# Retention and a Mish block on one core: when the weight sums are made, which staging buffers they share, and where the first block's stores stand in the queue

## The chip, the core and the metric

The kernel runs on one core of a Trainium2 chip. The core has five instruction streams that work side by side and wait for each other through semaphores: TensorE (PE in the profile; its weight loads are shown as PEld), VectorE (DVE), ScalarE (ACT), GpSimd (POOL) and SyncE (SP). Here SP does nothing but issue transfers, and 16 DMA engines carry them. The metric is the device time of one execution in microseconds (us); smaller is better. A kernel's time is the median of its runs.

## The reference, cut to what matters

A retention layer (linear attention with a decay for each head) runs over 4 batches of 768 tokens, 8 heads of 64. Its output is the input of a block with two weight matrices and the activation Mish between them.

```python
gamma = 1.0 - 2.0 ** (-5.0 - np.arange(H))
for t in range(S):
    state = gamma * state + einsum('bhd,bhe->bhde', k[:, :, t], v[:, :, t])
    y[:, :, t] = scale * einsum('bhd,bhde->bhe', q[:, :, t], state)
x = y.transpose(0, 2, 1, 3).reshape(3072, 512)
h = x @ w_in                       # 512 x 2048
g = h * np.tanh(softplus(h))       # Mish
out = g @ w_out                    # 2048 x 512
```

## The kernel before, in words

**Tiling.** The 3072 tokens are 24 chunks of 128. In a chunk the retention is done as attention under a mask (scores, mask, times V) plus the contribution of a running state. The chunks go in blocks: block 0 has four, the ten others two each (`BLOCKS`, line 39). A block has three parts: the retention of its chunks gives x, transposed (`xts`); then come the products with w_in and Mish (g, by 128 of the 2048 columns); then the products with w_out, whose results go through an output tile `osb` to memory. The retention of the next block is threaded into the products of this one.

**Sums instead of products.** Blocks 2 to 10 do both large products with seven block products in place of eight, and block 1 does so for its first one. This needs sums of weight blocks, made once on DVE: `wsum` of w_in (eight instructions of 128x512, line 581) and `tmat` of w_out (eight of 128x1024, lines 542 to 545, four for each half). Each block also needs sums of its own x (`x_sums`, lines 588 to 595, four on DVE) and of its own g (`gsum`).

**Order.** The order on every engine is written out by hand: `first_block`, then for each later block a dictionary of steps (`steps_of_half` for block 1, `steps_of` for the others), and in plain loops a `plan` from a unit's number to the work behind it. DVE work that has no fixed place is put in a list `late` and taken off it one by one (`some_late`).

**The first block.** SP issues, in this order, Q, K and V of chunks 0 to 3, the four slices of w_in (L150), the first three quarters of w_out (L154), loads for chunks 4 and 5, the last quarter of w_out in two halves (L159), and on. All weights come as float32 into staging buffers and are cast to float16: w_in by DVE (L165; one half slice by POOL), w_out by DVE (L175), its last quarter by ACT (L173). From unit 2 to 15 the loop does products with w_in (L490), from 16 to 31 with w_out (L512). In the second half stand the casts of Q and V on POOL (L322, L331) and of K on ACT (L327) for the coming chunks; the transposes of chunks 4 and 5 on PE, copied out of PSUM by DVE (`turn`, L366 to L370), which the scores (L379) of those chunks need; the mask (L385) and the state (L405, L410).

**Staging buffers.** The pool `rn_wstage` has four buffers under the tag `wt`, 8 KB a partition each, handed out in turn: first Q, the four slices of w_in, the four quarters of w_out, `wsum`, two `tmat`, and one `gsum`. A new owner waits until its predecessor has been read. The pool `rn_g` has two buffers under the tag `g`, for the g of blocks 1 on, and two under `g0`, for block 0's.

**Stores.** `g2_out` (L516) copies a finished product into an `osb` tile (L521 on DVE, L519 on ACT) and puts its store on a list, `stores`; `store_due(now)` issues on SP whatever is due (L181). There are five `osb` buffers. Block 0 fills four of them. Its stores are all issued at the step `end` of block 1's first product, behind `turn_and_load(a)`, which issues a transposition by DMA (L344) and three loads (L132). After the transposition by DMA of a chunk, the loads of the chunk two further on follow.

The functions that the change touches, and their callers:

Of the kernel before, what the change touches and what calls it, by code (L numbers as in the profile page):

```python
# [9 lines left out]
FP16 = mybir.dt.float16  # L10
FP32 = mybir.dt.float32
# [5 lines left out]
def kernel(  # L17
# [9 lines left out]
    nc = tc.nc  # L27
    B, H, S, D = q.shape
    d_model, d_ff = moe_w_in.shape
    P = 128  # L30
# [10 lines left out]
    NFB = d_ff // P  # L41
    NBP = d_model // P
    NSL = 4
    FPS = NFB // NSL
# [20 lines left out]
    wstage = ctx.enter_context(tc.tile_pool(name="rn_wstage", bufs=3))  # L65
    gp = ctx.enter_context(tc.tile_pool(name="rn_g", bufs=2))
    hp = ctx.enter_context(tc.tile_pool(name="rn_h", bufs=1))
    op = ctx.enter_context(tc.tile_pool(name="rn_o", bufs=5))
# [28 lines left out]
    for c in range(2):  # L97
        t = tri_first[c * HB:(c + 1) * HB]
# [16 lines left out]
    xts, gts, wins, wouts, wtmps = {}, {}, {}, {}, {}  # L115
# [29 lines left out]
    def load_w(which, s):  # L145
        if which == "in":
            t = wstage.tile([P, NBP, TB], FP32, name="wi", tag="wt", bufs=4)
            n = TB // 2 if s < 2 else TB
            for o in range(0, TB, n):
                nc.sync.dma_start(t[:, :, o:o + n], win_ap[:, :, s * TB + o:s * TB + o + n])  # L150
        else:
            t = wstage.tile([P, FPS, d_model], FP32, name="wt", tag="wt", bufs=4)
            if s < NSL - 1:
                nc.sync.dma_start(t, wout_ap[:, s * FPS:(s + 1) * FPS])  # L154
        wtmps[which, s] = t
# [6 lines left out]
    def cast_win(s, half, eng):  # L162
        src = wtmps["in", s]
        t = cpool.tile([P, NBP, TB // 2], FP16, name=f"win{s}_{half}")
        eng.tensor_copy(t, src[:, :, half * (TB // 2):(half + 1) * (TB // 2)])  # L165
        wins[s, half] = t

    def cast_wout(s, on_act=False):
# [6 lines left out]
            nc.vector.tensor_copy(t, src)  # L175
        wouts[s] = t

    def store_due(now):
        while stores and stores[0][0] <= now:
            _, dst, osb = stores.pop(0)  # L180
            nc.sync.dma_start(dst, osb)  # L181

# [341 lines left out]

    def weight_sums(half):
        n, hf = NFB // 2, d_model // 2  # L530
        if half == 0:
            tmats.extend(
                wstage.tile([P, 2, n, hf], FP16, name="tmat", tag="wt", bufs=4)
                for _ in range(2))
        f = slice(half * FPS, (half + 1) * FPS)
        t1, t2 = tmats[0][:, 0, f], tmats[0][:, 1, f]
        t3, t4 = tmats[1][:, 0, f], tmats[1][:, 1, f]
        b11, b12 = wouts[half][:, :, :hf], wouts[half][:, :, hf:]
        b21, b22 = wouts[half + 2][:, :, :hf], wouts[half + 2][:, :, hf:]
        sub = ALU.subtract  # L540
        return [
            lambda: nc.vector.tensor_tensor(t1, b12, b11, op=sub),
            lambda: nc.vector.tensor_tensor(t2, b22, t1, op=sub),
            lambda: nc.vector.tensor_tensor(t3, b22, b12, op=sub),
            lambda: nc.vector.tensor_tensor(t4, b21, t2, op=sub),
        ]

    def room_for_sums():
        n = NFB // 2
        gsums.append(wstage.tile([P, 4, n, P], FP16, name="gsum", tag="wt", bufs=4))  # L550
        gsums.append(gp.tile([P, 4, n, P], FP16, name="gsum", tag="g0"))

    def sum_views(blk, f=slice(None)):
        s = gsums[blk % 2]
# [236 lines left out]
    def first_block():  # L791
        qf = load_first_q()
        for s in range(2):
            for nm in "kv":
                for half in range(2):
                    load_two(nm, s, half)
        nload[0] = CPB
        load_weights()
        xts[0] = xtp.tile([P, CPB, HP, C], FP16, name="xt")

        at = at_tile()
        spin_wide(at, HP)
        spin_wide(at, HP)
        spin(at, 8)
        tq = turn_first_q(qf, 0)
        spin_wide(at, 3)
        first_q_out(0, tq, nc.scalar)
        tq = [tq, turn_first_q(qf, 1)]
        cast_two("k", 0, 0)
        turn_two(0, 0)  # L810
        first_q_out(1, tq[1], nc.vector)
        turned_two(0, 0)
        cast_two("k", 0, 1)
        spin_wide(at, 3)
        scores_half(0, 0, at)
        mask_half(0, 0, at)
        turn_two(0, 1)
        turned_two(0, 1)
        for half in range(2):
            cast_two("v", 0, half)  # L820
        at = at_tile()
        spin_wide(at, 3)
        scores_half(0, 1, at)
        mask_half(0, 1, at)
        cast_two("k", 1, 0)
        turn_two(1, 0)
        turned_two(1, 0)
        cast_two("k", 1, 1)
        outer_first(0)
        state_first(0)  # L830
        at = at_tile()
        scores_half(1, 0, at)
        mask_half(1, 0, at)
        y = atps.tile([P, 2, HP, C], FP32, name="y_ps", tag="at")
        present_first(0, y, range(HP))
        turn_two(1, 1)
        turned_two(1, 1)
        state_first(1)
        past_first(1, y)
        xt_out(0, y, nc.scalar, 2)  # L840
        for half in range(2):
            cast_two("v", 1, half)
        cast_win(0, 0, nc.gpsimd)
        at = at_tile()
        scores_half(1, 1, at)
        mask_half(1, 1, at)
        y = atps.tile([P, 2, HP, C], FP32, name="y_ps", tag="at")
        outer_first(1)
        state_first(2)
        present_first(1, y, range(HP // 2))  # L850
        h_ps = [mmps.tile([P, 1, TB], FP32, name="h_ps", tag="mm") for _ in range(2)]
        first_g1(h_ps[0], 0, 0)
        present_first(1, y, range(HP // 2, HP))
        past_first(2, y)
        past_first(3, y)
        xt_out(2, y, nc.scalar)
        xt_out(3, y, nc.vector)
        first_g1(h_ps[1], 1, 0)
        cast_win(0, 1, nc.vector)
        for u in range(2):  # L860
            first_g1(h_ps[u], u, 1)
            mish(0, u, h_ps[u])
        state_first(3)
        for s in range(1, NSL):
            for half in range(2):
                cast_win(s, half, nc.vector)
        plan = {
            9: [(cast_wout, 0)],
            12: [(cast_wout, 1)],
            16: [(cast_wout, 2), (load_more,), (casts, CPB)],  # L870
            23: [(casts, CPB + 1), (cast_wout, 3, True)],
            24: [(turn, CPB)],
            25: [(scores_one, CPB)],
            27: [(turn, CPB + 1)],
            28: [(outer_state, CPB), (casts, CPB + 2), (turn_and_load, CPB + 2), (cast_q, CPB + 3)],
            29: [(scores_one, CPB + 1)],
            31: [(y_two, 1)],
        }
        o_tiles = [None] * CPB
        for u in range(2, 2 * NFB):  # L880
            if u < NFB:
                g1(0, u)
            elif u < 2 * NFB - 2:
                w = u - NFB
                for t in range(CPB):
                    if w == 0:
                        o_tiles[t] = mmps.tile([P, d_model], FP32, name="o_ps", tag="mm")
                    g2_mm(o_tiles[t], 0, t, w)
            else:
                for t in range(CPB // 2) if u % 2 == 0 else range(CPB // 2, CPB):  # L890
                    for w in range(NFB - 2, NFB):
                        g2_mm(o_tiles[t], 0, t, w)
                    g2_out(o_tiles[t], 0, t, 1, on_act=t == CPB - 1)
            for fn, *args in plan.get(u + 1, ()):
                fn(*args)
            if u == NFB + 1:
                late.extend(win_sums())
            if NFB < u <= NFB + 4:
                late.pop(0)()
                late.pop(0)()  # L900
            if u == NFB + 4:
                late.extend(weight_sums(0))
            if u in (NFB + 5, NFB + 8):
                late.pop(0)()
        hsnaps.append(gp.tile([P, 4, TB], FP32, name="hsnap", tag="g0"))

    def turn_and_load(g):
# [43 lines left out]
            "m3": only((x_sums, nb)),  # L951
        }

    def some_late(n):
        for _ in range(min(n, len(late))):
            late.pop(0)()

    def steps_of_half(blk):
        a = first[blk] + 4
        return {  # L960
            "p2": [(gate_x, blk), (cast_v, a - 1)],
            "u2": [(cast_k, a - 1)],
            "p6": [(turn_and_load, a - 1), (some_late, 1)],
            "p7": [(cast_q, a), (some_late, 1)],
            "p4": [(cast_v, a), (some_late, 2)],
            "end": [(cast_k, a), (turn_and_load, a), (store_due, 3)],
        }

    def plan_of(blk):
# [6 lines left out]

    first_block()
    x_sums(HALF_SEVEN)
    late.extend(weight_sums(1))
    room_for_sums()  # L980
    for blk in range(1, len(BLOCKS)):
        if blk >= SEVEN:
            steps = steps_of(blk)
# [50 lines left out]
```

## Time and profile before

| what | value |
|---|---|
| median of 3 runs | 204.72 us (204.32 to 204.83) |
| the profiled execution's own time | 204.39 us |
| its span in the profile | 202.6 us |
| busy: PE, PEld, DVE, ACT, POOL | 193.1, 152.6, 143.5, 111.3, 67.6 us |
| granted TensorE clock | 1.00 |
| moved by DMA | 38.65 MB, mean 191 GB/s |

The profile shows one execution, a little under the median of the runs. The span is what the engines' records cover; 1.79 us of the time lie around it. A line of a timeline gives the start, the duration, the engine, the line of the kernel, the operation, what is written and read, and in brackets how long the engine was idle before it and what ended that wait. The releaser is inferred: it is the last one that the profile shows, which can be wrong where a DMA was waited for as well. Durations of one engine overlap a little, because the next instruction starts before the last one's results have all arrived.

### The profile page before, as it was taken

What the parts mean: (1) busy time and instruction counts of PE and PEld (TensorE: products, weight loads), DVE (VectorE), ACT (ScalarE), POOL (GpSimd) and SP (SyncE); (2) the same over time, 40 slices, a digit from 0 to 9 for tenths busy, and PEclk for the clock granted to TensorE, in tenths of its full rate; (3) what the DMA queues carried; (4) which work ended last, traced back from release to release, by engine and by line L of the source; (5) the groups of instructions that cost most, each with busy time, mean ns of one, the idle gap of its engine ahead of it and who ended that gap; (6) DMA issues with size and microseconds to landing.
All of it is one profiled execution on the core that took longest, in us unless ns stands there. A gap on an engine that the chain in (4) does not pass through costs nothing.

```text
span 202.6 us, 5428 instructions
## 1 busy us (share of the span) xinstructions
PE 193.1 (95%) x2239; PEld 152.6 (75%) x2239; DVE 143.5 (71%) x271; ACT 111.3 (55%) x199; POOL 67.6 (33%) x83
## 2 busy tenths in 40 slices
PE   6788999989999899999999999999999999999993
PEld 2355444445865788988988988988988988988982
DVE  2786644988889587578596696787696696696552
ACT  2462764152970673774674674674674663753850
POOL 4072000607434236424407517604407616200000
PEclk9999999999999999999999999999999999999999
DMA  5999999999999999997991992999992952200202
GB/s 175 300 314 359 386 387 297 275 250 199 188 172 223 326 217 206 188 239 149 230 186 55 222 240 80 230 180 155 248 210 48 234 87 55 104 3 23 85 26 78
DMA packets 95896, 38.65 MB, mean 191 GB/s; under 512 B 82304, under 2 KB 89984, under 8 KB 95872
## 3 DMA queue, kind: packets, MB, share of 16 engines
q1 hardware_dynamic: 92608, 37.50, 82.8%
q10 hardware_dynamic: 3264, 0.82, 2.4%
q8 instruction: 17, 0.28, 0.6%
q14 instruction: 7, 0.06, 0.1%
HBM read 27.30 MB, written 6.29 MB: 166 GB/s over the span
## 4 chain that ended last, share of the span: by engine, by line
PE 76%; DMA 10%; SPq 6%; DVE 4%; ACT 1%; issue 1%
PE o_ps L714 28%; PE h_ps L643 18%; PE h_ps L619 16%; PE o_ps L512 6%; DMA wi<-in_moe_w_in_dram 5%; DMA wt<-in_moe_w_out_dram 5%; SPq L217 4%; PE y_ps L429 3%; PE at L379 3%; DVE wsum L581 3%; PE y_ps L419 2%; SPq L150 2%; PE u_ps L393 2%; ACT xt L475 1%; DVE win L165 1%
## 5 line engine op out<-in xcount | busy, mean ns | idle before, releaser
L643 PE MATMUL h_ps<-xt,win 128*128 128x256 f16 x320 | 41.2, 273 | 0.0
L322 POOL TENSOR_TENSOR qk<-qf,qvs 128x512 f16<-128x512 f32 x20 | 23.4, 1172 | 26.2 <-DMA qf<-in_q_dram 26.2
L643 PEld LDWEIGHTS <-win 128*128 128x128 f16 x320 | 29.4, 98 | 3.6
L714 PEld LDWEIGHTS <-gsum 128*128 128x128 f16 x288 | 27.5, 98 | 3.9
L636 DVE TENSOR_TENSOR hsum<-h_ps,hsnap 128x512 f32<-128x512 f32 x30 | 19.8, 688 | 13.5 <-PE h_ps L619 11.3
L647 ACT ACTIVATE g<-h_ps 128x512 f16<-128x512 f32 x40 | 23.7, 594 | 5.6 <-PE h_ps L643 5.5
L385 DVE TENSOR_TENSOR am<-at,tri 128x1024 f16<-128x1024 f32 x20 | 24.2, 1216 | 1.6 <-PE at L379 1.6
L714 PE MATMUL o_ps<-tmat,gsum 128*128 128x256 f16 x216 | 25.1, 273 | 0.0
L626 ACT COPY hsnap<-h_ps 128x512 f32<-128x512 f32 x30 | 16.6, 588 | 14.5 <-PE h_ps L619 14.5
L331 POOL TENSOR_TENSOR v<-vf,qvs 128x512 f16<-128x512 f32 x20 | 21.5, 1073 | 5.4 <-DMA vf<-in_v_dram 5.4
L714 PEld LDWEIGHTS <-g 128*128 128x128 f16 x216 | 21.1, 98 | 2.5
L728 DVE TENSOR_TENSOR osb<-o_ps,snap 128x256 f32<-128x256 f32 x27 | 11.4, 423 | 16.1 <-PE o_ps L714 11.7
L512 PE MATMUL o_ps<-wout,g 128*128 128x512 f16 x96 | 22.7, 380 | 0.0
L475 ACT CAST xt<-y_ps 128x1024 f16<-128x1024 f32 x10 | 10.1, 1012 | 19.7 <-PE y_ps L429 19.7
L630 ACT ACTIVATE g<-hsum 128x512 f16<-128x512 f32 x30 | 18.7, 634 | 4.0 <-DVE hsum L636 4.0
L619 PEld LDWEIGHTS <-wsum 128*128 128x128 f16 x320 | 19.1, 98 | 1.1 <-DVE xsum L593 0.6
L720 ACT COPY snap<-o_ps 128x256 f32<-128x256 f32 x27 | 10.1, 373 | 15.7 <-PE o_ps L714 15.7
L327 ACT ACTIVATE qk<-kf 128x512 f16<-128x512 f32 x20 | 12.7, 633 | 9.4 <-DMA kf<-in_k_dram 5.0
L714 PE MATMUL o_ps<-wout,g 128*128 128x256 f16 x144 | 17.2, 273 | 0.0
L619 PE MATMUL h_ps<-xsum,wsum 128*128 128x128 f16 x240 | 16.7, 219 | 0.4 <-DVE xsum L593 0.4
L340 POOL COPY gate<-gsum 128x1 f16<-128x1 f16 x8 | 1.5, 188 | 44.0 <-DVE gsum L688 44.0
L619 PEld LDWEIGHTS <-win 128*128 128x128 f16 x240 | 15.1, 98 | 1.5 <-issue 0.8
(96 smaller groups left out, 288.5 us busy)
## 6 DMA issues: line engine op xcount, KB each, us to landing
kf<-in_k_dram SPq DMA_DIRECT2D x23, 256.0 KB, 3.9
vf<-in_v_dram SPq DMA_DIRECT2D x23, 256.0 KB, 5.5
out_dram<-osb SPq DMA_DIRECT2D x22, 256.0 KB, 4.3
qf<-in_q_dram SPq DMA_DIRECT2D x19, 256.0 KB, 4.4
wt<-in_moe_w_out_dram SPq DMA_DIRECT2D x3, 1024.0 KB, 8.8
wi<-in_moe_w_in_dram SPq DMA_DIRECT2D x4, 512.0 KB, 7.3
wi<-in_moe_w_in_dram SPq DMA_DIRECT2D x2, 1024.0 KB, 11.2
qfirst<-in_q_dram SPq DMA_DIRECT2D x2, 512.0 KB, 5.1
```

The lines of the kernel that those rows point to most:

```text
L322: nc.gpsimd.tensor_tensor(room16(g)[0], loaded[g][0], qs.unsqueeze(2).broadcast_to((P, H, D)), op=ALU.mult)
L327: nc.scalar.mul(room16(g)[1], loaded[g][1], BOOST)
L331: nc.gpsimd.tensor_tensor(room16(g)[2], loaded[g][2], vs.unsqueeze(2).broadcast_to((P, H, D)), op=ALU.mult)
L385: nc.vector.tensor_tensor(am, ats.pop(g), tri.unsqueeze(1).unsqueeze(1).broadcast_to((P, 2, HP, C)), op=ALU.mult)
L512: nc.tensor.matmul(o_ps, gts[blk, fb][:, t * P:(t + 1) * P], wouts[s][:, f, cols], start=(fb == 0), stop=(fb == NFB - 1))
L619: nc.tensor.matmul(h_ps[:, f], w(f, d), x(d), start=first and f == 0 and d == 0, stop=d == n - 1, skip_group_check=True)
L626: nc.scalar.copy(x, h_ps)
L630: nc.scalar.activation(gt[:, 2 * i * FPS:(2 * i + 1) * FPS, j * P:(j + 1) * P], h, AF.Mish, scale=inv_boost3)
L636: nc.vector.tensor_tensor(h, h_ps, x, op=ALU.add)
L643: nc.tensor.matmul(h_ps[:, j], win(s, 2 * half + j, bp), xt(blk, bp), start=bp == 0, stop=bp == NBP - 1)
L647: nc.scalar.activation(gt[:, fb:fb + 2], h_ps, AF.Mish, scale=inv_boost3)
L714: nc.tensor.matmul(o_ps, x(f), w(f), start=first and f == 0, stop=f == n - 1, skip_group_check=True)
```

## The change

In words:

- The eight sums of w_in (`wsum`) move from the second half of block 0 (units 17 to 20) to the casts of w_in: four behind slice 2, four behind slice 3. 
- The eight sums of w_out (`tmat`) start at unit 16: five of them in units 16 to 20 (before: one behind unit 21 and one behind unit 24), one at each of the steps `p6`, `p7` and `p4` of block 1 (before: four at these steps and two in the loop behind).
- Staging: quarters 2 and 3 of w_out are loaded into the two buffers `g` instead of `wt`. The order of owners in `wt` becomes first Q, four slices of w_in, two quarters of w_out, `wsum`, `gsum`, two `tmat`. The load of quarter 2 no longer waits for the cast of w_in's slice 2.
- Stores: block 0's four stores are issued two at step `p4`, ahead of `turn_and_load(a)`, and two behind it at step `end`, whatever their due number.

PE's instructions and their order stay as they were; POOL's and ACT's too. DVE's differ only by the moved sums, SP's by the two moved stores.

```diff
@@ load_w
-            t = wstage.tile([P, FPS, d_model], FP32, name="wt", tag="wt", bufs=4)
+            if s < NSL // 2:
+                t = wstage.tile([P, FPS, d_model], FP32, name="wt", tag="wt", bufs=4)
+            else:
+                t = gp.tile([P, FPS, d_model], FP32, name="wt", tag="g")
@@ stores
+    def store(n):
+        for _ in range(n):
+            _, dst, osb = stores.pop(0)
+            nc.sync.dma_start(dst, osb)
+
     def store_due(now):
         while stores and stores[0][0] <= now:
-            _, dst, osb = stores.pop(0)
-            nc.sync.dma_start(dst, osb)
+            store(1)
@@ sums
+    def some_late(n):
+        for _ in range(min(n, len(late))):
+            late.pop(0)()
...
     def room_for_sums():
         n = NFB // 2
         gsums.append(wstage.tile([P, 4, n, P], FP16, name="gsum", tag="wt", bufs=4))
-        gsums.append(gp.tile([P, 4, n, P], FP16, name="gsum", tag="g0"))
+
+    def room_for_more():
+        n, hf = NFB // 2, d_model // 2
+        tmats.extend(
+            wstage.tile([P, 2, n, hf], FP16, name="tmat", tag="wt", bufs=4) for _ in range(2))
@@ first_block
         for s in range(1, NSL):
             for half in range(2):
                 cast_win(s, half, nc.vector)
+            if s == 2:
+                late.extend(win_sums())
+            if s >= 2:
+                some_late(4)
+        room_for_sums()
...
-            if u == NFB + 1:
-                late.extend(win_sums())
-            if NFB < u <= NFB + 4:
-                late.pop(0)()
-                late.pop(0)()
-            if u == NFB + 4:
-                late.extend(weight_sums(0))
-            if u in (NFB + 5, NFB + 8):
-                late.pop(0)()
+            if u == NFB - 1:
+                room_for_more()
+                late.extend(weight_sums(0) + weight_sums(1))
+            if NFB <= u < NFB + 5:
+                some_late(1)
@@ steps_of_half
-            "p4": [(cast_v, a), (some_late, 2)],
-            "end": [(cast_k, a), (turn_and_load, a), (store_due, 3)],
+            "p4": [(cast_v, a), (some_late, 1), (store, 2)],
+            "end": [(cast_k, a), (turn_and_load, a), (store, 2)],
@@ behind first_block
     x_sums(HALF_SEVEN)
-    late.extend(weight_sums(1))
-    room_for_sums()
+    gsums.append(gp.tile([P, 4, NFB // 2, P], FP16, name="gsum", tag="g0"))
```

`weight_sums` computes the same four differences for a half as before; only its views are written as functions.

More of the change, by code (lines that the diff above doesn't have):

```diff
@@ L524, in g2_out, with t, b @@
         stores.append((due, dst, osb))
+    def some_late(n):
+        for _ in range(min(n, len(late))):
+            late.pop(0)()
     def weight_sums(half):
[L530 to L534, printed above, removed]
+        hf = d_model // 2
         f = slice(half * FPS, (half + 1) * FPS)
[L536 to L539, printed above, removed]
         sub = ALU.subtract
+        def t(i):
+            return tmats[i // 2][:, i % 2, f]
+        def b(i, j):
+            return wouts[half + 2 * i][:, :, j * hf:(j + 1) * hf]
         return [
[L542 to L545, printed above, removed]
+            lambda: nc.vector.tensor_tensor(t(0), b(0, 1), b(0, 0), op=sub),
+            lambda: nc.vector.tensor_tensor(t(1), b(1, 1), t(0), op=sub),
+            lambda: nc.vector.tensor_tensor(t(2), b(1, 1), b(0, 1), op=sub),
+            lambda: nc.vector.tensor_tensor(t(3), b(1, 0), t(1), op=sub),
         ]
@@ L952, in steps_of @@
         }
-    def some_late(n):
-        for _ in range(min(n, len(late))):
-            late.pop(0)()
     def steps_of_half(blk):
```

## The prediction

> **What bounds the kernel now.** I read the span first, then the engines' busy time by stretches, then what TensorE (PE) waited for, then the timeline around each such wait. In the rows by stretch the columns are: stretch, length, busy time (count) of PE, PEld, DVE, ACT and POOL, granted clock, DMA share, GB/s.
>
> ```profile
> span 202.6 us, 5428 instructions
> ...
> 20.00:33.00 13.00, 13.00 (x64) 6.08 (x63) 7.09 (x10) 8.86 (x16) 0.00 (x0) 1.00 1.06 381
> ...
> 40.00:46.00 6.00, 5.10 (x46) 2.83 (x44) 4.73 (x6) 2.72 (x3) 1.36 (x2) 1.00 1.20 252
> ...
> 67.00:75.00 8.00, 7.54 (x109) 6.76 (x109) 6.16 (x15) 5.86 (x11) 3.42 (x4) 1.00 1.17 279
> ...
> 90.00:190.00 100.00, 100.00 (x1274) 89.82 (x1273) 73.21 (x152) 59.65 (x111) 36.07 (x42) 1.00 0.74 146
> ```
>
> From 90 to 190 us PE never pauses, so only a pause that PE makes earlier can be won. The list of waits names two after 33 us, both on DVE:
>
> ```profile
> PE at L379 <- DVE qkt L370: 0.9, 1, 0.9
> PE h_ps L619 <- DVE xsum L593: 0.4, 1, 0.4
> ```
>
> The change touches both places. PE's own instructions stay the same, in the same order.
>
> **Sums of w_in, moved forward (eight wsum, L581).** They now stand behind the casts of slice 2 (four) and slice 3 (four).
>
> ```profile
> 20.71 12.25 PE L490 MATMUL h_ps<-xt,win 128*128 128x512 f16 x56
> 23.52 1.29 DVE L165 CAST win<-wi 128x1024 f16<-128x1024 f32 x2 [0.73 <-DMA wi<-in_moe_w_in_dram]
> 26.20 1.30 DVE L165 CAST win<-wi 128x1024 f16<-128x1024 f32 x2 [1.38 <-DMA wi<-in_moe_w_in_dram]
> 28.91 1.23 DVE L175 CAST wout<-wt 128x2048 f16<-128x2048 f32 x1 [1.42 <-DMA wt<-in_moe_w_out_dram]
> ...
> 34.45 1.23 DVE L175 CAST wout<-wt 128x2048 f16<-128x2048 f32 x1 [1.59 <-DMA wt<-in_moe_w_out_dram]
> 35.59 0.42 DVE L581 TENSOR_TENSOR wsum<-win 128x512 f16<-128x512 f16 x1
> ```
>
> One sum takes about 0.37 us from start to start (0.42 less the overlap), four about 1.5. DVE is idle for 1.38 us ahead of the casts of slice 3, and 1.42 ahead of wout0: the sums fill these gaps and push each cast by some 0.1. PE runs 56 matmuls from 20.71 in 12.25 us and wants slice 3 after 40 of them, at 29.5; its first cast ends near 27.0. So I take nothing. Bounds: a slowed sum takes 1.27 (below); four of those would end at 29.9 and the cast at 30.6, a PE pause of 1.1. POOL, which slows them, does nothing from 20 to 33 (row above), so I keep the low end.
>
> **Load of w_out's third part, no longer waiting for slice 2's cast.** SP may issue it up to 2 us sooner. But the rings are full from 20 to 33 us (share 1.06, 381 GB/s), one ring serves in order, and 1 MB at 381 GB/s is 2.75 us whenever it is queued. Gain 0; upper bound the 2 us that SP waited. The third cast then still starts at 34.45. The other shared buffers (sums, g) get earlier or equally early owners: their last readers are casts that DVE or ACT has done in block 0, before the next writer's turn. 0.
>
> **The first pause, 42 us.** Chunk 4's turned Q and K are copied by DVE (L370) before PE can score.
>
> ```profile
> 36.04 1.15 DVE L581 TENSOR_TENSOR wsum<-wsum,win 128x512 f16<-128x512 f16 x1
> 37.11 1.26 DVE L581 TENSOR_TENSOR wsum<-win,win 128x512 f16<-128x512 f16 x1
> ...
> 39.75 1.27 DVE L581 TENSOR_TENSOR wsum<-win,wsum 128x512 f16<-128x512 f16 x1
> 40.94 0.68 DVE L542 TENSOR_TENSOR tmat<-wout 128x1024 f16<-128x1024 f16 x1
> 41.54 0.68 DVE L370 COPY qkt<-t_ps 128x1024 f16<-128x1024 f16 x1
> ...
> 35.69 1.22 POOL L322 TENSOR_TENSOR qk<-qf,qvs 128x512 f16<-128x512 f32 x1 [19.04 <-DMA qf<-in_q_dram]
> 36.89 1.20 POOL L331 TENSOR_TENSOR v<-vf,qvs 128x512 f16<-128x512 f32 x1
> 39.64 1.10 POOL L322 TENSOR_TENSOR qk<-qf,qvs 128x512 f16<-128x512 f32 x1 [1.55 <-DMA qf<-in_q_dram]
> ...
> 40.12 0.39 PE L368 MATMUL t_ps<-ident,qk 128*128 128x128 f16 x4
> 40.34 1.03 PE L512 MATMUL o_ps<-wout,g 128*128 128x512 f16 x4
> 42.27 0.40 PE L379 MATMUL at<-qkt 64*128 64x128 f16 x8 [0.90 <-DVE qkt L370]
> ```
>
> PE's transposes end at 40.51, so the copy could start at 40.55 instead of 41.54, and PE score at 41.28 (0.73 after the copy's start, as 41.54 to 42.27): a gain of 0.99 if DVE is free by then. Eight wsum and one tmat leave the place behind the wout2 cast; five tmat take it. Free of POOL that is 5 x 0.6 = 3.0 us, done at 38.6.
>
> But the three long wsum are those that meet a POOL cast, and each ends 0.28 us after that cast (36.91 to 37.19, 38.09 to 38.37, 40.74 to 41.02): two-input DVE sums and POOL casts take turns. A tmat that waits so ends 0.28 + 0.27 (the doubled elements) = 0.55 after POOL. Played through: tmat 1 from 35.59 to 36.27, POOL's first cast to 37.18, tmat 2 to 37.73, POOL's second to 38.63, tmat 3 to 39.18, tmat 4 to 39.78; POOL's third arrives at 39.64, ahead of tmat 5, which starts near 39.7, so tmat 5 ends at 41.25. The copy starts at 41.17, PE at 41.90: gain 0.37. The bounds are 0 and 0.99, and some 60 ns at 39.64 decide; I take 0.37, since the rows show the turns.
>
> The Trainium skill, page "SBUF — State Buffer", section "Who interferes with whom", says that a DVE instruction with two SBUF inputs contends with a POOL instruction that reads SBUF, that the loser blocks for the whole instruction, and that issue order decides. By that rule, the first pause yields 0.37; without it, 0.99; the three long wsum agree with it.
>
> What follows a gain of 0.37:
>
> ```profile
> 46.37 1.04 POOL L322 TENSOR_TENSOR qk<-qf,qvs 128x512 f16<-128x512 f32 x1
> 46.80 1.16 DVE L410 TENSOR_TENSOR st<-su,gcm 128x512 f16<-128x512 f32 x1
> 47.88 1.21 DVE L385 TENSOR_TENSOR am<-at,tri 128x1024 f16<-128x1024 f32 x1
> 49.44 0.64 PE L429 MATMUL y_ps<-am,v 128*64 128x128 f16 x16
> ```
>
> The state update L410 waits for the POOL cast of 46.37 already; issued 0.37 sooner, at 46.43, it still does, so the mask behind it ends at 49.09 as before. PE would want it at 49.07 instead of 49.44, and gets it at 49.13 (0.04 to hand over). So 0.31 of the 0.37 stays.
>
> **The second pause, 69 us: the stores.** The output tiles (osb) have five buffers; block 0 takes four and block 1's second tile takes the first again, so its copy (L521) waits until the first store has landed.
>
> ```profile
> 63.44 0.85 SPq L181 DMA_DIRECT2D out_dram<-osb  x1
> out_dram<-osb SPq DMA_DIRECT2D x1, 256.0 KB, 4.2
> ...
> 65.84 1.04 PE L512 MATMUL o_ps<-wout,g 128*128 128x512 f16 x4
> 66.86 0.63 ACT L327 ACTIVATE qk<-kf 128x512 f16<-128x512 f32 x1
> 67.66 0.59 ACT L626 COPY hsnap<-h_ps 128x512 f32<-128x512 f32 x1 [0.17 <-PE h_ps L619]
> 67.69 0.69 DVE L521 COPY osb<-o_ps 128x512 f32<-128x512 f32 x1 [1.76 <-PE h_ps L619]
> 67.90 0.61 PE L393 MATMUL u_ps<-v,qk 128*128 128x128 f16 x8
> 68.96 1.07 PE L619 MATMUL h_ps<-xsum,wsum 128*128 128x128 f16 x16 [0.45 <-DVE xsum L593]
> ```
>
> The row puts the copy's wait down to PE, but 63.44 + 4.2 = 67.64 is the store, and DVE starts 0.05 later. Behind the copy stand the x sums, and PE waits for the second of them until 68.96. Its previous work, eight matmuls from 67.90 (0.45 at their spacing), lets it go on at 68.35: 0.61 to win. The new order issues the first two stores right after chunk 9's loads:
>
> ```profile
> 57.93 1.00 SPq L132 DMA_DIRECT2D vf<-in_v_dram  x1
> 59.18 1.84 SPq L344 DMA_TRANSPOSE qkt<-qk  x1
> 61.07 0.58 SPq L132 DMA_DIRECT2D kf<-in_k_dram  x1
> kf<-in_k_dram SPq DMA_DIRECT2D x1, 256.0 KB, 3.7
> ```
>
> That is near 59.0, landing near 63.2, over 3 us before block 1's last tile. The copy then starts when PE's last four matmuls end (66.88). From the copy's start to PE's it is 1.27 (67.69 to 68.96), so the sums are there at 68.15 and PE goes on at 68.35. I take 0.61; bounds 0 and 0.61.
>
> What pays are the queue's later entries: the transpose of chunk 8 (59.18) and chunk 10's three loads (from 61.07) each go behind two stores, 0.5 MB or some 1.2 us (four stores take 2.41 us of SP, half of them 1.2). The transpose is not needed before the next block's scores, past 73 us. Chunk 10's K is needed sooner: ACT casts it (L327, 66.86) straight ahead of the snapshot L626 that PE needs. It lands at 61.07 + 3.7 = 64.77 now. With 1.2 more it is 65.97, against a cast that is wanted at 66.55 after the first gain: hidden, with 0.6 to spare.
>
> The three tmat left for block 1 stand where six stood: 0.
>
> **The sum.** 204.39 (the profiled execution: span 202.6 and 1.79 around it) - 0.31 - 0.61 = 203.47. The median of the runs shown, 204.72, is 0.33 above that execution, which makes 203.80 at the median; the runs lie from 204.32 to 204.83, so I forecast between the two scales, 203.6.
>
> **The rivals.**
>
> *DVE gets past POOL.* If tmat 5 is issued before POOL's third cast (its Q lands 0.1 us later, or DVE runs 0.1 ahead), the first pause goes almost whole: 0.99 + 0.61 = 1.60, 202.8 on the profile's scale, 203.1 at the median. For it: only 60 ns are missing. Against it: the order is set by a DMA landing that the change does not touch. Chance 0.25.
>
> *Half comes.* The gain of one place only: tmat 5 caught for longer, or chunk 10's K landing between 66.6 and 67.8 and holding the snapshot. Gain 0 to 0.6, so 204.1 to 204.7. For it: the turns with POOL are tight, and the queue's backlog grows by two stores. Chance 0.22.
>
> *Chunk 10's K too late.* Its cast blocks ACT, the snapshot L626 starts 0.55 after the cast, and PE goes on 0.63 after that: landing + 1.18. From a landing of 67.8 on, PE starts no sooner than 68.96, and both gains are gone. Issued at 62.3 (61.07 + 1.2), it needs 5.5 us for that; 6.1 us makes 68.4 and +0.6, that is 205.0 (205.3 at the median). For it: the queue is full there. Against it: this load takes 3.7 now. Chance 0.08.
>
> **How the numbers follow.** The forecast has 0.45. A difference under 0.3% (0.61 us) can't be told from none here. Forecast and the first rival are faster, and a little of the second: 0.72. Most of the second is within: 0.19. The late K is slower, with what I have not thought of: 0.09. The range goes from the first rival on the profile's scale, 202.8, to well into the second, 204.5.
>
> **What would show it.** Right: no osb copy (L521) that waits over 1 us, first stores near 59, PE's wait at L619 gone, L379 reached near 41.9 with tmat 5 ending near 41.2, and the later blocks shifted as a whole. L379 at 41.3 is the first rival. Wrong: a DMA wait of ACT's K cast near 66 us with PE waiting for the snapshot; slice 3 cast after 29.5; the wout2 cast away from 34.4; a new PE pause between 46 and 67.

## The result, and the profile after

| | before | after |
|---|---|---|
| median | 204.72 us (203.76 to 205.47, 22 runs) | 203.91 us (203.0 to 204.49, 22 runs) |
| ratio after/before, 95% interval | | 0.9966 (0.9952 to 0.9979) |
| the profiled execution's own time | 204.39 us | 203.41 us |
| its span | 202.6 us | 201.2 us |

The changed kernel is faster by some 0.3%. The rows by stretch of the changed kernel, with the same columns as in the prediction:

```profile
40.00:46.00 6.00, 6.00 (x50) 3.17 (x48) 3.76 (x5) 2.48 (x3) 1.56 (x2) 1.00 1.19 251
67.00:75.00 8.00, 8.00 (x112) 7.25 (x110) 6.50 (x15) 5.91 (x11) 3.42 (x4) 1.00 1.11 253
```

PE is busy through both stretches (5.10 of 6.00 us and 7.54 of 8.00 before), and its list of waits holds nothing at L386 and L632, which are lines 379 and 619 of before. The timeline up to the first place (lines 168 and 178 are DVE's casts of w_in and w_out, 551 to 554 are the `tmat` sums, before 542 to 545; 377 is the copy, before 370; 329 and 338 are POOL's casts, before 322 and 331):

```profile
26.36 1.30 DVE L168 CAST win<-wi 128x1024 f16<-128x1024 f32 x2
29.08 1.23 DVE L178 CAST wout<-wt 128x2048 f16<-128x2048 f32 x1
...
34.60 1.23 DVE L178 CAST wout<-wt 128x2048 f16<-128x2048 f32 x1 [1.59 <-DMA wt<-in_moe_w_out_dram]
36.46 1.42 DVE L552 TENSOR_TENSOR tmat<-wout,tmat 128x1024 f16<-128x1024 f16 x1
37.80 1.53 DVE L553 TENSOR_TENSOR tmat<-wout,wout 128x1024 f16<-128x1024 f16 x1
39.25 0.68 DVE L554 TENSOR_TENSOR tmat<-wout,tmat 128x1024 f16<-128x1024 f16 x1
39.85 0.68 DVE L551 TENSOR_TENSOR tmat<-wout 128x1024 f16<-128x1024 f16 x1
40.40 0.39 PE L375 MATMUL t_ps<-ident,qk 128*128 128x128 f16 x4
40.52 1.04 POOL L329 TENSOR_TENSOR qk<-qf,qvs 128x512 f16<-128x512 f32 x1 [1.74 <-DMA qf<-in_q_dram]
40.82 0.69 DVE L377 COPY qkt<-t_ps 128x1024 f16<-128x1024 f16 x1 [0.29 <-PE t_ps L375]
41.58 0.40 PE L386 MATMUL at<-qkt 64*128 64x128 f16 x8
```

The second and third `tmat` take turns with POOL's casts as forecast (1.42 and 1.53 us instead of 0.68). The fifth takes only 0.68: in this execution POOL's third cast, which waits for its Q to land, starts at 40.52, where the profile of before had it at 39.64. PE's last transposes start 0.28 us later here than before (40.40 against 40.12), and the scores come at 41.58. So the profile shows the first rival, "DVE gets past POOL" (it had the scores at 41.28), while the median lies beside the forecast's own sum. That contradiction was the question for the experiments.

The second place, by the timeline of the changed kernel:

```profile
57.68 1.77 SPq L184 DMA_DIRECT2D out_dram<-osb  x2
...
66.16 0.63 ACT L334 ACTIVATE qk<-kf 128x512 f16<-128x512 f32 x1
66.22 0.69 DVE L528 COPY osb<-o_ps 128x512 f32<-128x512 f32 x1 [0.98 <-PE o_ps L519]
67.20 0.61 PE L400 MATMUL u_ps<-v,qk 128*128 128x128 f16 x8
67.65 1.06 PE L632 MATMUL h_ps<-xsum,wsum 128*128 128x128 f16 x16
```

The copy of the output tile (L528, before L521) waits for PE alone now, and PE goes from L400 to L632 without a pause.

### The profile page after: what moved, and what is told of

Its sections match the earlier page's. It is cut to its first block, busy times and chain, and to the rows that moved or that the text cites. A ratio compares the mean times of both kernels' runs of the same rounds, so it can differ in the third digit from the quotient of the medians.

```text
span 201.2 us, 5425 instructions
## 1 busy us (share of the span) xinstructions
PE 193.6 (96%) x2239; PEld 152.5 (76%) x2239; DVE 142.3 (71%) x271; ACT 111.2 (55%) x199; POOL 68.1 (34%) x83
## 4 chain that ended last, share of the span: by engine, by line
PE 91%; ACT 2%; DMA 2%; DVE 2%; issue 1%; DVEq 0%
PE o_ps L727 28%; PE h_ps L656 18%; PE h_ps L632 16%; PE o_ps L519 10%; PE h_ps L497 6%; PE y_ps L436 3%; PE at L386 3%; DMA qfirst<-in_q_dram 2%; PE y_ps L426 2%; PE u_ps L400 2%; ACT xt L482 1%; PE h_ps L800 1%; DVE qfirst L204 1%; DVE am L274 1%; ACT qk L235 1%
## 5 line engine op out<-in xcount | busy, mean ns | idle before, releaser
L329 POOL TENSOR_TENSOR qk<-qf,qvs 128x512 f16<-128x512 f32 x20 | 24.1, 1207 | 25.3 <-DMA qf<-in_q_dram 23.4
L741 DVE TENSOR_TENSOR osb<-o_ps,snap 128x256 f32<-128x256 f32 x27 | 11.4, 424 | 16.1 <-PE o_ps L727 11.3
L632 PEld LDWEIGHTS <-wsum 128*128 128x128 f16 x320 | 19.1, 98 | 0.5
L632 PE MATMUL h_ps<-xsum,wsum 128*128 128x128 f16 x240 | 16.7, 219 | 0.0
L632 PEld LDWEIGHTS <-win 128*128 128x128 f16 x240 | 15.1, 98 | 1.5 <-issue 0.8
```

The costliest lines, as they stand in the source:

```text
L329: nc.gpsimd.tensor_tensor(room16(g)[0], loaded[g][0], qs.unsqueeze(2).broadcast_to((P, H, D)), op=ALU.mult)
L632: nc.tensor.matmul(h_ps[:, f], w(f, d), x(d), start=first and f == 0 and d == 0, stop=d == n - 1, skip_group_check=True)
```

## The experiments

Three readings of each trace do most of the work, and need a word first. The *chain* is the time from the start of DVE's cast of w_out's third quarter (34.45 before, 34.60 after) to PE's first scores of chunk 4: DVE's work in between and, where DVE is done early, the wait for PE's transposes. The *turn* is the time from PE's transposes (L375) to those scores: PE's own view. The *second stretch* is the time from those scores to the first matmul on `xsum` (L632). What follows after that is the same in all: from L632 to the end of the span are 133.5 to 133.7 us (202.6 - 68.96 before, 201.2 - 67.65 after). Experiments are measured beside the kernel before on the same chip, on three chips in all, on which the kernel before has medians of 204.64, 204.81 and 204.89; so kernels of different chips are compared by their ratios. The columns in the middle come from the one profiled execution each, worked out from its rows.

| kernel | third POOL cast | chain | turn | second stretch | span | median of runs (range, runs) | ratio to before (95%) |
|---|---|---|---|---|---|---|---|
| before | 39.64 | 7.82 | 2.15 | 26.69 | 202.6 | | |
| after | 40.52 | 6.98 | 1.18 | 26.07 | 201.2 | 203.91 (203.0 to 204.49, 22) | 0.9966 (0.9952 to 0.9979) |
| stores_only | 40.38 | 7.22 | 1.18 | 26.08 | 201.4 | 203.91 (203.08 to 204.47, 12) | 0.9960 (0.9936 to 0.9984) |
| six_osb | 39.81 | 7.83 | 2.40 | 26.08 | 202.4 | 204.22 (202.97 to 204.48, 12) | 0.9975 (0.9954 to 0.9996) |
| sums_only | 39.69 | 7.44 | 1.73 | 27.05 | 202.8 | 204.85 (204.03 to 205.32, 12) | 1.0003 (0.9982 to 1.0023) |
| load_only | 39.82 | 7.83 | 2.43 | 26.85 | 203.3 | 204.96 (204.44 to 205.44, 12) | 1.0013 (0.9996 to 1.0031) |
| four_stores_early | 39.58 | 7.43 | 1.65 | 26.07 | 201.6 | 204.00 (203.32 to 205.29, 12) | 0.9976 (0.9951 to 1.0002) |
| after_again | 39.49 | 7.44 | 2.09 | 26.07 | 201.8 | 203.92 (203.74 to 204.84, 12) | 0.9972 (0.9955 to 0.9989) |
| four_first | 39.88 | 6.09 | 1.18 | 26.08 | 200.9 | 203.15 (202.75 to 203.57, 8) | 0.9931 (0.9901 to 0.9960) |
| pool_gate | 40.87 | 6.89 | 1.18 | 26.08 | 201.3 | 203.24 (202.81 to 203.29, 6) | 0.9927 (0.9904 to 0.9949) |
| four_old_stores | 39.43 | 6.54 | 1.18 | 27.03 | 201.8 | 203.91 (203.63 to 203.99, 5) | 0.9949 (0.9931 to 0.9967) |
| stores_gate | 41.01 | 6.98 | 1.46 | 26.08 | 201.2 | 203.11 (203.08 to 203.29, 4) | 0.9916 (0.9892 to 0.9939) |

**The stores alone** (stores_only). The kernel before, with the new order of the stores and nothing else of the change.

```diff
-            "p4": [(cast_v, a), (some_late, 2)],
-            "end": [(cast_k, a), (turn_and_load, a), (store_due, 3)],
+            "p4": [(cast_v, a), (some_late, 2), (store, 2)],
+            "end": [(cast_k, a), (turn_and_load, a), (store, 2)],
```

> The kernel before, with only the stores of block 0 issued two by two. My theory: the copy L521 waits for the landing of the first store, so its idle 1.8 us goes, PE's 0.45 us wait for the x sums at 69 us goes, and the first pause (PE at L379 waiting for the copy L370 near 42 us) stays: 0.6 us less than before, ratio 0.997. Rival (the row is right, the copy waits for PE): nothing changes, ratio 1.000. Rival (chunk 10's K comes too late behind the stores): ACT's cast near 66 us waits for a DMA and PE for the snapshot; ratio 1.000 or above.

Measured 0.9960 (0.9936 to 0.9984): as much as the whole change. The second stretch is 26.08 us, 0.61 less than before. The timeline of this kernel shows something that was not expected:

```profile
40.09 0.69 DVE L546 TENSOR_TENSOR tmat<-wout 128x1024 f16<-128x1024 f16 x1
40.38 1.29 POOL L326 TENSOR_TENSOR qk<-qf,qvs 128x512 f16<-128x512 f32 x1 [2.30 <-DMA qf<-in_q_dram]
40.91 0.69 DVE L374 COPY qkt<-t_ps 128x1024 f16<-128x1024 f16 x1
41.66 0.40 PE L383 MATMUL at<-qkt 64*128 64x128 f16 x8
```

The *old* order of the sums makes no pause here either. POOL's third cast came at 40.38, behind all eight `wsum`, and none of the last was caught. So the first pause isn't a property of the old order alone: in the profiles of the old order it is there where POOL's third cast starts by 39.82 (before, six_osb, load_only), and missing here.

**A sixth output buffer** (six_osb). The kernel before with six `osb` buffers, so that no copy needs an early store; room for it comes from the first chunks' Q, which takes its buffer from the pool's common tag. No engine's order changes.

```diff
-    op = ctx.enter_context(tc.tile_pool(name="rn_o", bufs=5))
+    op = ctx.enter_context(tc.tile_pool(name="rn_o", bufs=6))
...
-        q16 = castp.tile([P, CPB, n, D], FP16, name="qfirst16", bufs=1, tag=f"qfirst16_{half}")
+        q16 = castp.tile([P, CPB, n, D], FP16, name="qfirst16", tag="qk16")
```

> The kernel before, every instruction the same, but six osb buffers instead of five (two cast buffers of the start are taken from another pool's rotation to make room). If the copy L521 waits for the first store to leave its buffer, its wait goes without any store being moved: 0.6 us less, ratio 0.997, PE's wait at 69 us gone. If the copy waits for PE, as the row puts it, ratio 1.000.

Measured 0.9975 (0.9954 to 0.9996). The timeline of this kernel, and its list of waits:

```profile
63.92 2.76 SPq L181 DMA_DIRECT2D out_dram<-osb  x4
67.45 0.69 DVE L521 COPY osb<-o_ps 128x512 f32<-128x512 f32 x1 [0.98 <-PE o_ps L512]
```

```profile
PE at L379 <- DVE qkt L370: 1.2, 1, 1.2
```

The stores are issued as late as before, yet the copy waits for PE alone, the second pause is gone, and the second stretch is 26.08 us. This shows that it was the buffer, held by its store, that made the pause, and not PE, which the row of before named as the releaser.

**The sums and the staging alone** (sums_only). The changed kernel with the stores where they were.

```diff
-            "p4": [(cast_v, a), (some_late, 1), (store, 2)],
-            "end": [(cast_k, a), (turn_and_load, a), (store, 2)],
+            "p4": [(cast_v, a), (some_late, 1)],
+            "end": [(cast_k, a), (turn_and_load, a), (store_due, 3)],
```

> The changed kernel with the stores as before, all four at the step end. My theory: the first pause goes wholly or in part, 0.3 us (the fifth tmat caught behind POOL's third cast) to 1.0 us (not caught); the second pause at 69 us stays or grows, because PE now comes sooner to a store that lands as late as before: if the store's landing hangs on SP's queue and not on PE, some of the first gain is taken back there. Ratio 0.996 to 0.999. Rival (both gains are DVE's order alone): as fast as the changed kernel, 0.9966.

Measured 1.0003 (0.9982 to 1.0023): no gain, and less than the expected 0.996 to 0.999. The timeline of this kernel, both places:

```profile
39.69 1.21 POOL L329 TENSOR_TENSOR qk<-qf,qvs 128x512 f16<-128x512 f32 x1 [0.84 <-DMA qf<-in_q_dram]
39.92 1.53 DVE L551 TENSOR_TENSOR tmat<-wout 128x1024 f16<-128x1024 f16 x1
...
42.11 0.40 PE L386 MATMUL at<-qkt 64*128 64x128 f16 x8 [0.47 <-DVE qkt L377]
...
63.50 2.53 SPq L184 DMA_DIRECT2D out_dram<-osb  x4
67.88 0.69 DVE L528 COPY osb<-o_ps 128x512 f32<-128x512 f32 x1 [2.12 <-DMA out_dram<-osb]
69.16 0.34 PE L632 MATMUL h_ps<-xsum,wsum 128*128 128x128 f16 x3 [0.81 <-DVE xsum L606]
```

The fifth `tmat` is caught behind POOL's cast, as the forecast said. The chain is 7.44 us instead of 7.82, so 0.38 is won there; it began 0.22 later, so the scores come 0.16 sooner. But PE comes to the second place at 69.16, where it came at 68.96. The stores went out at 63.50, no sooner than before (63.44), and the copy waits for the first to land. PE's wait there grew from 0.45 to 0.81: the second pause takes what the first one gave. Here the profile itself names the store as the releaser.

**The load alone** (load_only). The kernel before, with quarters 2 and 3 of w_out staged in the buffers `g`.

```diff
-            t = wstage.tile([P, FPS, d_model], FP32, name="wt", tag="wt", bufs=4)
+            if s < NSL // 2:
+                t = wstage.tile([P, FPS, d_model], FP32, name="wt", tag="wt", bufs=4)
+            else:
+                t = gp.tile([P, FPS, d_model], FP32, name="wt", tag="g")
```

> The kernel before with only the staging of w_out's third and fourth quarter changed (buffers g instead of wt); sums and stores as before. My theory: the rings are full and serve in order, so the third quarter's cast starts as before, near 34.5, and the time stays, ratio 1.000 (0.998 to 1.002). Rival (the load comes sooner and all of w_out with it): the cast starts up to 2 us sooner, ratio 0.997 or below.

Measured 1.0013 (0.9996 to 1.0031). Its timeline and its list of waits:

```profile
34.98 1.23 DVE L178 CAST wout<-wt 128x2048 f16<-128x2048 f32 x1 [1.59 <-DMA wt<-in_moe_w_out_dram]
68.38 0.69 DVE L524 COPY osb<-o_ps 128x512 f32<-128x512 f32 x1 [1.92 <-DMA out_dram<-osb]
```

```profile
PE at L382 <- DVE qkt L373: 1.2, 1, 1.2
```

The third quarter's load was issued 1.35 us sooner (23.50 against 24.85 before), as the edit allows, but it took 11.4 us to land instead of 9.6, and the quarter is not there sooner (34.98 against 34.45). six_osb, which doesn't touch this load, has 34.98 too, so this start differs between executions by half a microsecond, whatever the staging, and the first pause follows it: 1.2 us at 34.98, 0.9 at 34.45.

**All four stores early** (four_stores_early). The changed kernel with the second pair of stores ahead of the loads as well: twice the load on SP's queue.

```diff
-            "p4": [(cast_v, a), (some_late, 1), (store, 2)],
-            "end": [(cast_k, a), (turn_and_load, a), (store, 2)],
+            "p4": [(cast_v, a), (some_late, 1), (store, 4)],
+            "end": [(cast_k, a), (turn_and_load, a)],
```

> The changed kernel with all four stores of block 0 at the step p4, so that four stores (1 MB) instead of two stand ahead of the transposition of chunk 8 and the loads of chunk 10. It prices my slower rival. Two more stores put K of chunk 10 some 1.2 us later, landing near 66.5 to 67.2, against a cast that ACT wants at 66.2: a wait of 0.3 to 1.0 us on ACT, of which PE loses what exceeds its small slack: 0.2 to 0.9 us slower than the changed kernel, ratio to before 0.998 to 1.001. If K lands in time all the same, the ratio stays 0.9966.

Measured 0.9976 (0.9951 to 1.0002). From its timeline:

```profile
57.91 2.69 SPq L184 DMA_DIRECT2D out_dram<-osb  x4
62.40 0.95 SPq L132 DMA_DIRECT2D kf<-in_k_dram  x1
66.52 0.63 ACT L334 ACTIVATE qk<-kf 128x512 f16<-128x512 f32 x1
```

Chunk 10's K goes out at 62.40 instead of 61.07 and lands 4.1 us later, at 66.50; ACT's cast starts at 66.52, with no wait in front of it. The second stretch is 26.07 us, as after. So in the profiled execution even twice the dose is hidden, but with nothing to spare. Five of the twelve runs took 204.45 to 205.29 us, three of them longer than any run of the changed kernel (at most 204.84). None of the five was profiled, and the ratio's interval reaches 1, so whether they paid the price that the slower rival set on the queue is open.

**The changed kernel again** (after_again), unedited, for a second profile.

> The changed kernel once more, for a second profile and more runs beside the other kernels. My theory: where chunk 5's Q lands before the fifth tmat is issued, the tmat takes 1.5 us and PE's scores start 1.7 us after the transposes; where it lands later, 0.68 and 1.2. The time, 203.4 to 204.5, goes with that. Ratio 0.9966.

Measured 203.92 us, 0.9972 (0.9955 to 0.9989). Its timeline:

```profile
34.68 1.23 DVE L178 CAST wout<-wt 128x2048 f16<-128x2048 f32 x1 [1.59 <-DMA wt<-in_moe_w_out_dram]
39.49 1.42 POOL L329 TENSOR_TENSOR qk<-qf,qvs 128x512 f16<-128x512 f32 x1 [0.63 <-DMA qf<-in_q_dram]
39.94 1.53 DVE L551 TENSOR_TENSOR tmat<-wout 128x1024 f16<-128x1024 f16 x1
...
42.12 0.40 PE L386 MATMUL at<-qkt 64*128 64x128 f16 x8 [0.84 <-DVE qkt L377]
...
59.18 1.27 SPq L184 DMA_DIRECT2D out_dram<-osb  x2
66.70 0.63 ACT L334 ACTIVATE qk<-kf 128x512 f16<-128x512 f32 x1
```

The same kernel, the other case: Q lands early, the fifth `tmat` is caught, PE waits 0.84 us. The scores come 2.09 us after the transposes and not the expected 1.7, since the transposes came sooner (40.03). The first stores leave at 59.18 here; chunk 10's K goes out at 61.95 and lands 4.2 us later, at 66.15, which is 0.55 ahead of its cast on ACT.

**Four sums in place of five** (four_first). The changed kernel; the fifth `tmat` comes later, so that nothing of DVE's stands behind POOL's third cast.

```diff
-            if NFB <= u < NFB + 5:
+            if NFB <= u < NFB + 4:
```

> The changed kernel with four tmat instead of five ahead of the copy L377; the fifth goes to block 1. My theory: DVE and POOL take turns, and whether the fifth tmat is caught behind POOL's third cast hangs on when that cast's Q lands. With four the copy always starts when PE's transposes end, so PE's scores follow 1.4 us after the transposes in every execution: 0 to 0.6 us less than the changed kernel in the median, ratio to before 0.994 to 0.9966. Rival (the spread of the changed kernel's runs comes from elsewhere): ratio 0.9966 as the changed kernel.

Measured 203.15 us, 0.9931 (0.9901 to 0.9960): faster than before, and its highest run, 203.57, lies below the median of stores_only on the same chip (203.91). The interval overlaps that of the changed kernel (0.9952 to 0.9979) a little. Its timeline:

```profile
39.88 1.46 POOL L329 TENSOR_TENSOR qk<-qf,qvs 128x512 f16<-128x512 f32 x1 [0.59 <-DMA qf<-in_q_dram]
40.03 0.39 PE L375 MATMUL t_ps<-ident,qk 128*128 128x128 f16 x4
40.45 0.69 DVE L377 COPY qkt<-t_ps 128x1024 f16<-128x1024 f16 x1
41.21 0.40 PE L386 MATMUL at<-qkt 64*128 64x128 f16 x8
```

Q lands early again (39.88), with no effect: the copy stands behind the transposes at once, and takes 0.69 us beside POOL's cast.

**A gate on POOL** (pool_gate). The changed kernel with all five sums, and ahead of POOL's third cast a copy of one column out of the fifth `tmat`, which makes POOL wait for it. It fixes the turn; PE's, DVE's, ACT's and SP's orders stay.

```diff
-            23: [(casts, CPB + 1), (cast_wout, 3, True)],
+            23: [(lambda: gate(tmats[0][:, 0, FPS, :1]),), (casts, CPB + 1), (cast_wout, 3, True)],
```

> The changed kernel with one more POOL instruction, a copy of one column that reads the fifth tmat's output, ahead of POOL's cast of chunk 5's Q, so that this cast can't start before the fifth tmat is done. DVE keeps all five tmat ahead of its copy. My theory: what delays the copy is the turn that POOL's cast takes, not the length of DVE's list; with the turn taken away PE's scores follow 1.2 us after its last transposes in every execution (as in the changed kernel's profile, 40.40 to 41.58), and the time is that of four_first, 203.2, ratio 0.993. Rival (five tmat are simply too much work ahead of the copy, or the changed kernel's spread has another source): ratio 0.9966 as the changed kernel, with the copy still late.

Measured 203.24 us, 0.9927 (0.9904 to 0.9949). Its timeline:

```profile
39.99 0.68 DVE L551 TENSOR_TENSOR tmat<-wout 128x1024 f16<-128x1024 f16 x1
40.73 0.19 POOL L347 COPY gate<-tmat 128x1 f16<-128x1 f16 x1 [1.81 <-DVE tmat L551]
40.87 1.04 POOL L329 TENSOR_TENSOR qk<-qf,qvs 128x512 f16<-128x512 f32 x1
40.88 0.69 DVE L377 COPY qkt<-t_ps 128x1024 f16<-128x1024 f16 x1 [0.20 <-PE t_ps L375]
41.63 0.40 PE L386 MATMUL at<-qkt 64*128 64x128 f16 x8
```

Q was issued at 33.78 and landed 6.0 us later, near 39.8, so it is the gate that holds POOL's cast until 40.87. The fifth sum takes 0.68, and the kernel gains 0.68 us on the changed one on the same chip (203.92 - 203.24). All six of its runs, from 202.81 to 203.29, lie below all twelve of after_again, from 203.74 to 204.84.

**Four sums, the stores as before** (four_old_stores). The two edits of four_first and sums_only together: the first pause gone, the second left in place.

```diff
-            if NFB <= u < NFB + 5:
+            if NFB <= u < NFB + 4:
...
-            "p4": [(cast_v, a), (some_late, 1), (store, 2)],
-            "end": [(cast_k, a), (turn_and_load, a), (store, 2)],
+            "p4": [(cast_v, a), (some_late, 1)],
+            "end": [(cast_k, a), (turn_and_load, a), (store_due, 3)],
```

> four_first (four tmat ahead of the copy) with all four stores at the step end, as before. If the two pauses are independent, the first gain stays: 0.7 us less than before at the median, ratio 0.9965. My theory since sums_only: the first store lands when SP's queue lets it, near 67.8, whatever PE does, so PE that comes sooner waits longer for the x sums, and the first gain is taken back there but for what SP's queue itself moves forward: ratio 0.998 to 1.000.

Measured 0.9949 (0.9931 to 0.9967): a miss for the account in which the second pause takes back all that the first gives. Its timeline:

```profile
41.19 0.40 PE L386 MATMUL at<-qkt 64*128 64x128 f16 x8
62.48 2.66 SPq L184 DMA_DIRECT2D out_dram<-osb  x4
66.95 0.69 DVE L528 COPY osb<-o_ps 128x512 f32<-128x512 f32 x1 [2.10 <-DMA out_dram<-osb]
68.22 1.07 PE L632 MATMUL h_ps<-xsum,wsum 128*128 128x128 f16 x16 [0.80 <-DVE xsum L606]
```

PE is 1.08 us earlier at the scores (42.27 - 41.19) and 0.74 at the second place (68.96 - 68.22). The stores went out 0.96 sooner here (62.48 against 63.44): they stand behind a transposition that itself follows the first place, so they move with most of a large gain. In sums_only, with a gain of 0.16 at the scores, they did not move. The rows show where that gain went: SP issued the transposition ahead of chunk 9's loads 0.17 sooner than before (54.22 against 54.39), but the issue took 2.64 us instead of 2.25, and the loads went out at 56.91 instead of 56.68. In four_old_stores it was issued at 53.30 and took 1.25. Why its length differs so is open.

**The stores and the gate, without the sums and the staging** (stores_gate). The kernel before with the edit of stores_only, and the gate on POOL against the first `tmat`, the last sum ahead of the copy there.

```diff
-            23: [(casts, CPB + 1), (cast_wout, 3, True)],
+            23: [(lambda: gate(tmats[0][:, 0, 0, :1]),), (casts, CPB + 1), (cast_wout, 3, True)],
```

> The kernel before with block 0's stores two by two, all sums and staging as before, and one POOL instruction that reads the first tmat's output ahead of POOL's cast of chunk 5's Q. Now my theory is that the first pause is a matter of POOL's turn alone. In stores_only's profile, where that cast came late by itself (40.38), the old order had no pause: tmat ended at 40.78, the copy started at 40.91. So the old order of sums with the turn taken away is as fast as pool_gate: 203.2, ratio 0.993. Rival (the sums have to move for the copy to be on time): between stores_only and pool_gate, ratio 0.995 to 0.996, with DVE's list ending after PE's transposes.

Measured 203.11 us, 0.9916 (0.9892 to 0.9939): as fast as anything here, with the sums in their old place. Its timeline:

```profile
40.12 0.68 DVE L546 TENSOR_TENSOR tmat<-wout 128x1024 f16<-128x1024 f16 x1
40.72 0.68 DVE L374 COPY qkt<-t_ps 128x1024 f16<-128x1024 f16 x1
41.01 1.04 POOL L326 TENSOR_TENSOR qk<-qf,qvs 128x512 f16<-128x512 f32 x1
41.46 0.40 PE L383 MATMUL at<-qkt 64*128 64x128 f16 x8 [0.21 <-DVE qkt L374]
```

DVE gets through all its sums by 40.80 when POOL lets it; of the first pause 0.21 us is left. Q had landed near 39.3 here (issued at 33.33, 6.0 us to landing), so it is the gate again that holds the cast.

## Why the prediction was right, point by point

**The sums of w_in: nothing, as forecast.** They fill DVE's gaps ahead of the casts. In the profile after, slice 3's casts start at 26.36 instead of 26.20, and wout0's at 29.08 instead of 28.91. Neither row has a wait in its brackets any more, so DVE came to them with no idle time: the gaps are full, and PE has no wait there. The feared price (POOL slowing them) was not met.

**The earlier load: nothing, as forecast.** load_only shows it by itself: what the load gains at its issue (1.35 us) it loses on its way (1.8 us).

**The first pause: the chain was right to 0.02 us, its basis was one execution.** The forecast played the turns through: from 34.45 to 41.90, a chain of 7.45. The three profiles in which the fifth `tmat` was caught have 7.44, 7.44 and 7.43. That the chain began at 34.60 in the profile after, which the forecast had named as a sign against itself, is none: under the old order it began between 34.44 (stores_only) and 34.98 (six_osb, load_only). A sum that is caught ends 0.55 us after the cast, as assumed (39.33 after 38.78 in the profile after, 41.47 after 40.91 in after_again). The forecast said that some 60 ns at 39.64 decide; the runs show that what decides is not 60 ns but where Q lands, and that moves between 39.4 and 40.5 from one execution to the next. Of four profiles with five `tmat` in this place and no gate, three were caught and one (after) was free, which agrees with the chance of 0.25 that the first rival had, as far as four can. What the forecast did not see is that the same holds for the *old* order: in stores_only it is free, too (caught in the profiles of before, six_osb and load_only). Where Q lands late, the old order loses nothing here, and the moved sums have nothing to win. Where it lands early, the rows bear the forecast's gains out: from the cast's start to the first matmul on `xsum` it is 34.51 us before and 33.51 in after_again.

**What follows it: no loss at the mask.** The forecast took off 0.06 there. In after_again PE reaches the same point, the matmuls of L436, 7.16 us after the scores (49.28 - 42.12), before 7.17 (49.44 - 42.27).

**The second pause: right to 0.01 us.** Forecast 0.61; the second stretch falls from 26.69 to 26.07 in both profiles of the changed kernel, and six_osb takes the same 0.61 by another way. The first store landed in time with over 3 us to spare, and the copy waits for PE.

**What the queue pays: right in the case that was forecast.** The forecast had the first stores near 59.0, chunk 10's K landing at 65.97, and 0.6 us to spare before its cast. In after_again, where the fifth `tmat` is caught as forecast, they are 59.18, 66.15 and 0.55. In the profile after, where it is not caught, the queue comes sooner: the stores leave at 57.68 and K goes out at 60.97, where it was 61.07 before. In no profile does ACT's cast of that K wait for its landing, so the slower rival did not come about; four_stores_early shows that two more stores use up what was to spare.

**The sum.** 204.72 - 0.92 = 203.80 at the median was the forecast's own sum; 203.91 and 203.92 were measured. The 203.6 came from placing the time between the profiled execution's scale and the median's. That step was off: what is forecast is a median, and the sum made at the median misses it by 0.11, the one on the profiled execution's scale (203.47) by 0.44. That 203.80 lies so near is in part luck: the sum takes every execution to have Q early, while of the four profiles without a gate that each order has (five `tmat` ahead of the copy, or the old order), one has it late. The first rival's time at the median, 203.1, was met as well, by kernels in which DVE always gets past POOL: 203.24 with the gate, 203.15 with four sums.

**What the runs say of the parts.** Stores alone give 0.9960, sums and staging alone 1.0003, both 0.9966 and 0.9972. The stores alone give as much as the whole change. The moved sums shorten the chain by 0.38 us where Q lands early; in the time of the whole kernel their gain can't be told from none here, and the intervals leave room for the 0.31 of the forecast as well. So the 0.61 of the sum is shown by the times and the rows, the 0.31 by the rows alone.

## What to carry to other kernels

Before work is moved off an engine to end a stall, ask whether the work itself is too long or whether it is caught in a turn with a neighbour; here a gate of one column (203.92 to 203.24 us) did more than moving the sums, whose own gain the times don't show, and if a transfer's landing decides who goes first, one profile shows only one of the cases. A releaser in a row can be the wrong one: put the landing of a buffer's store beside the wait, and test it with one buffer more. And a gain ahead of a wait for a store can end in that wait, wholly (sums_only: 0.16 us ahead at the scores, 0.20 behind at the next place) or in part (four_old_stores: 1.08 ahead, then 0.74), so the later wait is worth removing first.

## What the hardware showed that was not expected

**The turns cost both sides, and only some instructions take part.** A two-input sum on DVE takes 0.68 us alone and 1.41 to 1.53 beside a POOL cast. The cast takes 1.04 alone, and longer where it starts while such a sum runs, by what is then left of the sum less 0.13 to 0.15 us: with 0.57 left it takes 1.46 (four_first), with 0.52 left 1.42 (after_again), with 0.31 left 1.21 (sums_only), with 0.20 left 1.10 (before). The copy out of PSUM takes 0.69 in four_first while POOL's cast runs from 39.88 to 41.34, and 0.69 in pool_gate beside a cast that keeps its 1.04. The Trainium skill, page "SBUF — State Buffer", section "Who interferes with whom", says that a DVE instruction with at most one SBUF input is free of the conflict outside the two fast modes that use both ports; these rows agree. So it matters which of DVE's instructions stands behind POOL's, and a copy out of PSUM may.

**One landing moves by a microsecond between executions of the same kernel.** POOL's third cast got its Q at 40.52 in one profile of the changed kernel and at 39.49 in the other, and the whole span differs by 0.6 us (201.2 and 201.8). This Q, chunk 5's, is not issued by SP, as the text ahead of the prediction has it, but on ACT's queue, as are chunk 4's K and chunk 5's V: at 33.72 and 33.36, landing 6.7 and 6.1 us later. In all twelve profiles the landing goes with an order between the two queues. Where Q came late (after, stores_only), SP issued the next part of w_out no later than ACT's queue issued the V behind that Q (34.36 and 34.36; 34.31 and 34.44); in the other ten SP was later, in four_stores_early by only 0.02 (34.27 and 34.25). No run forces this order, so that it makes the landing move is not shown.
